# Attention and a three-way-max layer: batch 1's probabilities left unnormalised, q left unscaled, narrower last score blocks, a new order

## The chip, the cores and the metric

The kernel runs on one core of one Trainium2 chip. The metric is the device time of one execution in microseconds (us), median of three runs.

## The reference

Four batches of causal attention, 12 heads of 64 over 448 positions, feed a layer that multiplies the tokens with three 768x768 matrices, takes the maximum of the three, and multiplies with a fourth.

```python
scores = scale * np.matmul(q, k.transpose(0, 1, 3, 2))      # scale = 1/8, q and k: 4 x 12 x 448 x 64
scores = np.where(mask, -1000000000.0, scores)
scores = scores - np.max(scores, axis=-1, keepdims=True)
attn = np.exp(scores)
attn = attn / (np.sum(attn, axis=-1, keepdims=True) + 1e-09)
x = np.matmul(attn, v)                                      # rearranged to 1792 tokens x 768
h = np.maximum(np.maximum(x @ w1, x @ w2), x @ w3)
out = h @ w_out
```

All inputs and outputs are float32.

## The kernel before

Work on the attention goes by *pairs* of heads: batch b has pairs 6b to 6b + 5, and `staging` and `attend` (L680, L705) add the steps of one. `staging` loads q and k, and a second copy of parts of them with the two heads exchanged, and multiplies q by 0.125 (L699, on POOL or ACT). `attend` cuts the causal triangle into two score halves (`HALVES`), each a bank of PSUM (S, two buffers). For each half:

- PE writes the masks (bf16) and the scores (float32) with 64x64 tiles, four at a time (L724);
- DVE takes the negated maxima of two groups of blocks (L768);
- ACT takes the exp of each block with its maximum as bias, and adds up the row's sum (L780).

Then the batches part. **Batch 0** is "plain" (`PLAIN = 6` pairs): PE transposes the exps (L794), ACT copies them back, PE multiplies with v in float32 (L877), and the division comes after that. DVE takes reciprocals of the sums (L891, L892), PE copies ("spreads") them over the rows of an M bank (L898, L903), ACT evicts that (L526, hacc<-M,bsc), and DVE multiplies it with the product (`quotient`, L906). **Batches 1 to 3** divide before: the sums are scaled on ACT or DVE (`eps`, L808 or L810), DVE takes reciprocals (L814), and each of seven blocks is multiplied by its own (`sc`; L526 on ACT, L528 on DVE). Then the probabilities are split into a float16 number (`p_hi`, ACT mostly, 1024 columns) and a float16 remainder (`p_lo`, L537, POOL or DVE); SP's DMA transposes both, and PE multiplies them with v, which is split likewise (L865). In all batches the result x is split into two float16 parts (x hi, x lo).

Beside this run the layer's steps. `weight` clamps each block of the weights (ACT |w| L989, DVE L974 to L986), `split` splits it (L526 or L530, L546 or L548 and L549), `hidden` multiplies batches 0 and 1 with it (L1066, three M banks) and takes the maximum in ACT's eviction and DVE's L1081. Batches 2 and 3 go through seven products in place of eight (L1298, L1423). The projection of batches 0 and 1 is L1477.

Which step comes when, and on which engine, is set by two tables at the top of the file. `ORDER` lists the steps' numbers in the order of issue; `ENGINE` has two letters for each step. Both were found by a search with the planner in `Order.forward`, which prices each step and follows the clock of PE (`pace`, `BUSY`). Every engine runs its instructions strictly in this order. A step of POOL is made to wait for the DVE step before it if that is marked `port=True`; a DVE step is never made to wait for POOL. `RINGS` gives the number of buffers of each kind (q and k three each, hacc four, M three).

Of the kernel before, what the change touches and what calls it, by code (L numbers as in the profile page):

```python
# [7 lines left out]
F32 = mybir.dt.float32  # L8
# [7 lines left out]
P = 128  # L16
D = 64
# [9 lines left out]
PS = 2.0**14  # L27

# [6 lines left out]
ORDER = [17, 15, 0, 16, 18, 19, 47, 49, 20, 30, 21, 2, 22, 31, 23, 24, 32, 25, 50, 4, 33, 6, 34, 7, 1, 3, 26, 51, 35, 27,  # L35
# [145 lines left out]


HALVES = (
    ((4, 0, 1, 0, 384, 0), (5, 1, 1, 512, 384, 512), (0, 2, 1, 384, 128, 384), (1, 3, 1, 896, 128, 896)),
    ((2, 4, 1, 0, 256, 0), (3, 5, 1, 512, 256, 256), (6, 6, 2, 256, 256, 512)),
)

# [1422 lines left out]
```

## Time and profile before

| | before |
|---|---|
| median of 3 runs | 455.88 us (454.98 to 456.64) |
| profiled execution | 456.02 us |
| its span, first to last instruction | 454.2 us |
| busy: PE, DVE, ACT, POOL | 430.0, 415.4, 311.6, 137.1 us |
| mean granted clock | 0.989 |

The profile is of one execution; its span is the time between the first and the last instruction on the engines, and 1.8 us of the execution lie outside it. A row of the trace names the line, the engine, the operation, what it writes and reads, and its size. A line can be that of a helper: L526, L528 and L530 are the scaled copies of ACT, DVE and POOL, L537 the subtraction for a float16 remainder. "idle before" is time in which the engine did nothing just before such a row, with what ended it. The granted clock is a share of TensorE's full speed of 2.4 GHz. In time, batch 0's attention takes about the first 69 us, the first hidden matmul is at 69.63 us, batches 1 to 3 with the layer's first part follow until 312 us, then the seven products until 435 us, and the last projections.

### The profile page before, as it was taken

To read this page: it belongs to the slowest core of one execution; us is meant where nothing else is said; L and a number is where in the kernel's file an instruction comes from. 1 tells how busy PE (TensorE), PEld (TensorE's weight loads), DVE (VectorE), ACT (ScalarE), POOL (GpSimd) and SP (SyncE) were. 2 spreads that over 40 slices of the span, in tenths; PEclk is the share of its full clock that TensorE was granted. 3 is DMA by queue.
4 is the path that set the end of the run, shared out by engine and by line. 5 is a ranking of instruction groups with operands and counts; after the bars stand their busy time and mean duration, and the time that the engine had idled before them with its cause. 6 is when DMAs were issued, how large, how long until landed. Compare 5 with 4: busy or idle time off the path is not lost.

```text
span 454.2 us, 11040 instructions
## 1 busy us (share of the span) xinstructions
PE 430.0 (95%) x4277; PEld 252.6 (56%) x4277; DVE 415.4 (91%) x824; ACT 311.6 (69%) x738; POOL 137.1 (30%) x118
## 2 busy tenths in 40 slices
PE   7878878879999999999999999999999999999996
PEld 4766754435555555565666566655555555555553
DVE  2798999999999999998878999889999999999984
ACT  2899999988998989997675688883443253332510
POOL 2013433415443441722333335521123022132000
PEclk9898999989999999999999999999999999999999
DMA  7768868897889978948986687853100000000014
GB/s 216 226 206 256 261 232 217 233 224 161 207 206 176 235 249 236 202 101 173 187 166 140 137 174 143 144 114 69 42 1 0 1 1 1 1 1 20 19 43 182
DMA packets 110003, 63.62 MB, mean 140 GB/s; under 512 B 81280, under 2 KB 107392, under 8 KB 109952
## 3 DMA queue, kind: packets, MB, share of 16 engines
q1 hardware_dynamic: 101312, 50.87, 47.7%
q10 hardware_dynamic: 8640, 12.06, 8.5%
q8 instruction: 33, 0.54, 0.5%
q14 instruction: 18, 0.15, 0.1%
HBM read 38.54 MB, written 5.51 MB: 97 GB/s over the span
## 4 chain that ended last, share of the span: by engine, by line
PE 69%; ACT 12%; DVE 12%; DMA 2%; issue 2%; SPq 1%; ACTq 0%
PE M L1066 16%; PE L L1298 14%; PE M L1477 9%; PE M L1298 7%; PE S L724 6%; ACT region L526 5%; PE O L865 5%; PE L L1423 4%; ACT region L780 3%; PE O L1298 3%; PE M L1423 2%; DVE region L974 2%; DVE acc L768 2%; DVE region L982 2%; PE O L1423 2%
## 5 line engine op out<-in xcount | busy, mean ns | idle before, releaser
L1066 PE MATMUL M<-x,w 128*128 128x448 f16 x648 | 129.4, 356 | 3.9 <-DVE hacc L1081 3.2
L780 ACT ACTIVATE region<-S,acc 128x384 f32<-128x384 f32 (+3 forms) x168 | 83.1, 502 | 24.3 <-DVE acc L768 14.5
L1066 PEld LDWEIGHTS <-w 128*128 128x128 f16 x648 | 61.9, 99 | 62.7 <-issue 8.3
L537 POOL TENSOR_TENSOR region<-region 128x1024 f16<-128x1024 f32 x27 | 57.6, 2133 | 82.0 <-ACT region L526 26.4
L768 DVE TENSOR_REDUCE acc<-S 128x2 f32<-128x512 f32 (+3 forms) x96 | 63.0, 681 | 13.1 <-PE S L724 12.8
L526 ACT ACTIVATE region<-region 128x1024 f16<-128x1024 f32 (+3 forms) x59 | 45.8, 786 | 22.8 <-DVE region L1231 9.2
L526 ACT ACTIVATE region<-region,acc 128x384 f32<-128x384 f32 (+3 forms) x99 | 48.2, 525 | 6.7 <-DVE acc L814 4.4
L526 ACT ACTIVATE region<-region,cols 128x384 f16<-128x384 f32 (+1 forms) x38 | 22.8, 614 | 42.0 <-DVE region L1156 20.3
L1151 POOL TENSOR_TENSOR region<-w 128x384 f32<-128x384 f16 x21 | 19.3, 921 | 96.0 <-DVE region L546 40.7
L1298 PEld LDWEIGHTS <-region 128*128 128x128 f16 x324 | 31.7, 98 | 29.6
L724 PE MATMUL S<-region 64*64 64x256 f32 (+5 forms) x672 | 47.2, 372 | 0.7 <-DMA region<-in_k_dram 0.5
L1477 PE MATMUL M<-h,w 128*128 128x448 f16 x216 | 42.9, 353 | 0.0
L1298 PE MATMUL L<-region,region 128*128 128x448 f16 x198 | 39.4, 352 | 0.0
L1298 PEld LDWEIGHTS <-w 128*128 128x128 f16 x243 | 23.5, 98 | 21.8
L780 ACT ACTIVATION_READ_ACCUMULATOR region<-S,acc 128x1 f32 x168 | 34.4, 205 | 0.0
L1298 PE MATMUL M<-x,w 128*128 128x448 f16 x162 | 33.6, 353 | 0.0
L724 PEld LDWEIGHTS S<-region 64*64 64x64 f32 x672 | 30.4, 138 | 5.2 <-POOL region L530 0.6
L1477 PEld LDWEIGHTS <-w 128*128 128x128 f16 x216 | 20.7, 98 | 19.2 <-issue 0.3
L865 PEld LDWEIGHTS <-region 128*64 128x64 f16 x1080 | 26.4, 111 | 5.0 <-issue 4.2
L865 PE MATMUL O<-region,region 128*64 128x128 f16 (+1 forms) x1080 | 28.9, 211 | 0.0
L989 ACT ACTIVATE region<-region 128x768 f32<-128x768 f32 x24 | 22.0, 920 | 3.2 <-DMA region<-in_moe_w_out_dram 1.3
L974 DVE TENSOR_SCALAR_CACHE_REDUCE region<-region 128x768 f32<-128x768 f32 x24 | 22.5, 941 | 1.7 <-ACT region L989 1.6
(177 smaller groups left out, 779.6 us busy)
## 6 DMA issues: line engine op xcount, KB each, us to landing
region<-in_moe_w_dram SPq DMA_DIRECT2D x13, 768.0 KB, 4.7
region<-in_q_dram SPq DMA_DIRECT2D x22, 224.0 KB, 4.1
region<-in_v_dram SPq DMA_DIRECT2D x11, 384.0 KB, 5.3
region<-in_k_dram SPq DMA_DIRECT2D x18, 224.0 KB, 3.7
region<-in_moe_w_dram ACTq DMA_DIRECT2D x5, 768.0 KB, 5.1
region<-in_moe_w_out_dram ACTq DMA_DIRECT2D x3, 768.0 KB, 5.1
region<-in_moe_w_out_dram SPq DMA_DIRECT2D x3, 768.0 KB, 4.7
out_dram<-osb SPq DMA_DIRECT2D x9, 224.0 KB, 2.9
```

What stands on the lines that cost most here:

```text
L526: ACT.activation(o, i, AF.Copy, scale=f)
L537: ENG[eng].tensor_tensor(out=o, in0=i, in1=hi, op=ALU.subtract)
L724: PE.matmul(ap(o, 512 * h + dims[0], dims[1:], D * g, D), l, r, start=start, stop=True, skip_group_check=True)
L768: DVE.tensor_reduce(out=T(acc)[:, at : at + len(g)], in_=i, op=ALU.max, axis=AX.XY if parts == 2 else AX.X, negate=True)
L780: ACT.activation(o, part(T(S), parts, c, w), AF.Exp, bias=T(acc)[:, at : at + 1], accum_out=T(acc)[:, 7 + at : 8 + at])
L865: PE.matmul(T(O)[D * h : D * h + D, P * i : P * i + w], vt[j][:, vl, (2 * p + h) * D : (2 * p + h + 1) * D], queries(T(pT[u]), i, h, 8 * p ...
L974: DVE.tensor_scalar(out=T(x32), in0=T(x32), scalar1=MIN_HI, scalar2=None, op0=ALU.max, op1=ALU.max, accum_out=wmx[:, c])
L989: add([("act", c_act(DM, 0.025))], lambda e: ACT.activation(T(x32), word(1).bitcast(F32), AF.Abs), reads=[st], writes=[x32], ring=("w3", x ...
L1066: PE.matmul(T(M)[:, 0:S_LEN], w16[j][:, kk, wl, fs], xx[:, kk % 3, xl], start=(kk == 0 and wl + xl == 0), stop=(kk == 5 and wl == 1))
L1298: PE.matmul(T(M)[:, 0:S_LEN], stat(c, wl), mov(c, xl), start=first and n == 0, stop=n == 8, skip_group_check=True)
L1423: PE.matmul(T(M)[:, 0:S_LEN], stat[0](c, wl), mov[0](c, xl), start=first and c + wl + xl == 0, stop=c == 2 and wl == 1, skip_group_check=True)
L1477: PE.matmul(T(M)[:, 0:S_LEN], w16[3][:, f, wl, es], T(("h", b, f))[:, hl], start=(f == 0 and hl + wl == 0), stop=(f == 5 and wl == 1))
```

## The change

1. q is no longer scaled. The exp has `scale=0.125`, and its bias is prepared by a new small step per half (`bias`, 48 in all: 19 on ACT, 15 on POOL, 14 on DVE), between max and exp. The bias also holds ln 2^14.
2. Batch 1 leaves its exps unnormalised as batch 0 does. Its `eps`, reciprocals and seven scalings per pair are gone; reciprocals of the sums, a spread on PE, ACT's eviction and DVE's quotient per pair come in, behind the float16 product with v.
3. The last block of the second half has 224 keys for each head in place of 256 and 192. Its exp is 448 wide in place of 512, the half's p hi and p lo 960 in place of 1024; the masks follow.
4. q and k take one load each per pair; the exchanged copies come by four loads for every second pair (`kx`). The rings of q and k have two buffers; quotients have one of their own (`xr`) in place of one in the ring of hacc.
5. The planner follows the clock with a second, shifted window, and its limit is 3900 in place of 3060. `ORDER` and `ENGINE` are new throughout. Among other things 18 in place of 13 weight blocks (w hi) are scaled on ACT, and 15 in place of 9 remainders of probabilities are taken on DVE.

The core of the diff:

```diff
 RINGS = dict(
-    qr=3, kr=3, kx=1, acc=2, p32=2, ph=2, pT=3, v16=5, vr=4, w3=4, x=4, wst=2, h=6, hacc=4, osb=2, S=2, O=1, M=3,
+    qr=2, kr=2, xr=1, kx=1, acc=2, p32=2, ph=2, pT=3, v16=5, vr=4, w3=4, x=4, wst=2, h=6, hacc=4, osb=2, S=2, O=1, M=3,
...
-    BUSY = 3060
+    BUSY = 3900
...
-                rate = 2400 if cols.get(k - 1, 0.0) >= self.BUSY else 1200
+                rate = 2400 if min(cols.get(k - 1, 0.0), shifted.get(m - 1, 0.0)) >= self.BUSY else 1200
...
-        def scale(e):
-            scaled(e, T(qr), T(qr), 0.125)
...
-        add(c_scaled("q", 512), scale, writes=[qr], prio=prio, port=True)
...
                 for h, g in tiles:
-                    rows(h, g, 2 + (h != g), 0, 192 + D * (h != g))
+                    rows(h, g, 2 + g, 0, 192 + D * g)
                 for h, g in tiles:
                     hs = slice(D * h, D * h + D)
                     if h == g:
-                        m(h, g, (256, [1, 256]), qq[hs, 384:448], kk[hs, 0:256])
+                        m(h, g, (256, [1, 224]), qq[hs, 384:448], kk[hs, 224 * h : 224 * h + 224])
                     else:
-                        m(h, g, (256, [1, 192]), qq[hs, 448:512], T(kz)[hs, :])
+                        m(h, g, (256, [1, 224]), T(kz)[hs, p % 2, 0:D], T(kz)[hs, p % 2, D : D + 224])
...
+            def bias(e, z=z):
+                dims = [[4, 2], [2, 2]] if z == 0 else [[2, 3]]
+                i, o = ap(T(acc), z, dims), ap(T(acc), 16 + z, dims)
+                if e == "act":
+                    ACT.activation(o, i, AF.Identity, bias=tiny[:, 0:1], scale=0.125)
+                else:
+                    ENG[e].tensor_scalar(out=o, in0=i, scalar1=0.125, scalar2=LN_PS, op0=ALU.mult, op1=ALU.add)
+
+            add([("act", 0.19), ("dve", 0.1), ("pool", 0.2)], bias, reads=[(acc, "m", z, gi) for gi in range(2)],
+                writes=[(acc, "b", z)], prio=pr)
...
-                        o, part(T(S), parts, c, w), AF.Exp, bias=T(acc)[:, at : at + 1],
-                        accum_out=T(acc)[:, 7 + at : 8 + at])
+                        o, part(T(S), parts, c, w), AF.Exp, bias=T(acc)[:, 16 + at : 17 + at], scale=0.125,
+                        accum_out=T(acc)[:, 8 + at : 9 + at])
...
+            own = [(y, bl[0], "e") for bl in blocks]
+            if b > 1:
...
+        if b > 1:
+            f = bsc[:, b, 11:12]
...
+        f = bsc[:, b, 10:11] if plain else 1.0
+        add([("dve", 0.38)], reciprocals, reads=[(acc, "s", n) for n in range(7)], writes=[(acc, "r")], prio=prio + 0.4)
+        add([("pe", 4 * c_pe32(P) + 0.09)], spread, reads=[(acc, "r")], writes=[R], ring=("M", R), prio=prio + 0.5, mode=(2, 3))
```

The steps `eps`, its reciprocal and `sc` stand unchanged under `if b > 1`; `reciprocals`, `spread` and `quotient` are those of batch 0 and run for batches 0 and 1. Line numbers after it: max L765, bias L775 (ACT) and L777, exp L789, product with v in batch 0 L894 and later L882, reciprocals L929 and L930, spread L936 and L941, quotient L944, hidden matmul L1083, its maximum L1098, scaled copy on ACT L527, subtraction L538, clamps L991 to L1003.

PE at the end of batch 0's attention, before: the last pair's scores, its spread and its product with v, then the first hidden matmul (L1066). S and M are PSUM banks, region_61 holds probabilities, region_64 v.

```order
402 L724 MATMUL S_92<-region_65 64x64
403 L898 MATMUL M_89<-ident,acc_68 64x128 x6
404 L903 MATMUL M_89<-ident,acc_68 64x64 x2
405 L877 MATMUL O_88<-region_61,region_64 64x128 x12
406 L877 MATMUL O_88<-region_61,region_64 64x64 x8
407 L1066 LDWEIGHTS w_1_95
408 L1066 MATMUL M_90<-x_69,w_1_95 128x448
```

The same place in the change. The hidden matmuls (L1083) begin after the scores of pair 7's second half, ahead of the last product with v of batch 0:

```order
423 L1083 LDWEIGHTS w_0_93
424 L1083 MATMUL M_90<-x_68,w_0_93 128x448
425 L894 MATMUL O_87<-region_61,region_64 64x128 x12
426 L894 MATMUL O_87<-region_61,region_64 64x64 x8
427 L1083 LDWEIGHTS w_0_93
428 L1083 MATMUL M_90<-x_68,w_0_93 128x448
```

Twelve hidden matmuls now stand ahead of this product with v (L894); before, it (L877) stood ahead of all of them.

ACT in batch 1, before: scalings by a column of reciprocals (region_61<-region_61,acc_68) between evictions, and then p hi (1024 wide).

```order
170 L526 ACTIVATE region_61<-region_61,acc_68 128x128
171 L526 ACTIVATE region_61<-region_61,acc_68 128x256
172 L526 ACTIVATE h_73<-hacc_81 128x448
173 L955 DMA region_62<-in_moe_w_dram 128x6x256
174 L526 ACTIVATE region_61<-region_61,acc_68 128x512
175 L526 ACTIVATE region_61<-region_61,acc_68 128x384
176 L526 ACTIVATE region_61<-region_61 128x1024
177 L526 ACTIVATE region_61<-region_61,acc_68 128x256
```

ACT in batch 1, in the change: exps (L789), p hi straight behind them, then the copy of x (x_70<-region_65) and the eviction of spread sums (region_65<-M_89).

```order
159 L789 ACTIVATE region_61,acc_66<-S_91,acc_66 128x256 x2
160 L789 ACTIVATE region_61,acc_66<-S_91,acc_66 128x448
161 L527 ACTIVATE hacc_81<-M_90,wr 128x448
162 L789 ACTIVATE region_61,acc_66<-S_92,acc_66 128x128
163 L527 ACTIVATE region_61<-region_61 128x1024
164 L972 DMA region_62<-in_moe_w_dram 128x6x256
165 L527 ACTIVATE h_74<-hacc_80 128x448
166 L527 ACTIVATE x_70<-region_65 128x448
167 L527 ACTIVATE region_64<-region_63,bsc 128x768
168 L527 ACTIVATE region_61<-region_61 128x960
169 L527 ACTIVATE region_65<-M_89 128x448
```

The scalings have gone from between exp and p hi; the eviction of spread sums and the copy of x from region_65, before and after the quotient, are new here.

DVE around the first hidden matmuls, before: the last max of a half, `eps` of the other half (L810) and the accumulation of a hidden product (L1081).

```order
154 L986 SCALAR_TENSOR_TENSOR region_62<-region_62 128x768
155 L974 TENSOR_SCALAR region_62,wmx<-region_62 128x768
156 L768 TENSOR_REDUCE acc_67<-S_93 128x1
157 L810 TENSOR_SCALAR acc_67<-acc_67,osc 128x4
158 L1081 SCALAR_TENSOR_TENSOR hacc_82<-M_89,wr,hacc_82 128x448
159 L814 RECIPROCAL acc_67<-acc_67 128x4
160 L768 TENSOR_REDUCE acc_68<-S_92 128x2
```

DVE at about the same place in the change: a quotient (L944), a clamp step, and the addition and reciprocal of eight sums (L929, L930).

```order
150 L765 TENSOR_REDUCE acc_66<-S_92 128x1
151 L944 TENSOR_TENSOR region_65<-O_87,region_65 128x448
152 L995 TENSOR_SCALAR region_62<-region_62 128x768
153 L929 TENSOR_SCALAR acc_67<-acc_67 128x8
154 L930 RECIPROCAL acc_67<-acc_67 128x8
155 L999 SCALAR_TENSOR_TENSOR region_62<-region_62 128x768
156 L547 SCALAR_TENSOR_TENSOR w_2_95<-region_62,wf,w_2_95 128x6x128
```

`eps` is no longer ahead of L1081; a quotient and a 128x8 addition stand between the maxima and the clamps in its place.

POOL in batch 1, in the change: remainders of probabilities, now 1024 and 960 wide by turns, then the bias of a half (L777) and a remainder of x.

```order
34 L654 MEMSET region_64 64x1536
35 L538 TENSOR_TENSOR region_61<-region_61 128x1024
36 L538 TENSOR_TENSOR region_61<-region_61 128x960
37 L777 TENSOR_SCALAR acc_66<-acc_66 128x3
38 L538 TENSOR_TENSOR x_70<-region_65,x_70 128x448
```

The bias stands behind the two remainders in POOL's queue; before there was none on POOL.

## Rows read from the trace of the kernel before

**Rows 1.** The page: engines' busy time and share; granted clock in 40 slices.

```profile
PE 430.0 (95%) x4277; PEld 252.6 (56%) x4277; DVE 415.4 (91%) x824; ACT 311.6 (69%) x738; POOL 137.1 (30%) x118
...
PEclk9898999989999999999999999999999999999999
```

**Rows 2.** Windows: stretch, length, busy of PE, PEld, DVE, ACT, POOL, clock, DMA share, GB/s.

```profile
0.00:107.00 107.00, 87.09 (x1088) 59.76 (x1088) 93.17 (x193) 94.14 (x240) 33.29 (x37) 0.95 0.79 226
107.00:435.00 328.00, 327.48 (x3115) 185.05 (x3110) 309.28 (x609) 215.91 (x496) 103.81 (x82) 1.00 0.51 113
```

**Rows 3.** Windows around two falls of the granted clock.

```profile
34.00:38.00 4.00, 4.00 (x43) 2.80 (x42) 3.94 (x11) 3.36 (x11) 2.52 (x4) 0.57 0.93 335
...
99.00:103.00 4.00, 4.00 (x14) 1.72 (x13) 4.00 (x11) 4.00 (x12) 0.00 (x0) 0.57 0.69 133
```

**Rows 4.** Waits of PE up to 107 us: total, times, longest.

```profile
PE S L724 <- ACT region L780: 5.4, 5, 1.9
PE M L1066 <- DVE hacc L1081: 2.8, 1, 2.8
PE M L794 <- ACT region L780: 2.2, 3, 1.4
...
PE M L794 <- ACT region L526: 1.9, 2, 1.2
```

**Rows 5.** Timelines of POOL, DVE, PE, 96 to 104 us: start, duration, row [idle before].

```profile
96.02 2.12 POOL L537 TENSOR_TENSOR region<-region 128x1024 f16<-128x1024 f32 x1 [5.41 <-ACT region L526]
...
96.23 1.93 DVE L810 TENSOR_SCALAR acc<-acc,osc 128x4 f32<-128x4 f32 x1
...
102.58 0.22 DVE L810 TENSOR_SCALAR acc<-acc,osc 128x3 f32<-128x3 f32 x1
...
98.80 5.25 PE L1066 MATMUL M<-x,w 128*128 128x448 f16 x18 [2.80 <-DVE hacc L1081]
```

**Rows 6.** Groups on ACT: line, operation, out<-in, count | busy, mean ns | idle before.

```profile
L526 ACT ACTIVATE region<-region,acc 128x384 f32<-128x384 f32 (+3 forms) x99 | 48.2, 525 | 6.7 <-DVE acc L814 4.4
...
L526 ACT ACTIVATE w<-region,wf 128x768 f16<-128x768 f32 x13 | 11.8, 938 | 0.3 <-DVE wf L593 0.3
...
L526 ACT ACTIVATE region<-region 128x512 f32<-128x512 f32 x12 | 7.6, 633 | 0.0
...
L526 ACT ACTIVATE hacc<-M,bsc 128x448 f32<-128x448 f32 x6 | 3.9, 642 | 1.2 <-PE M L903 1.2
...
L808 ACT ACTIVATE acc<-acc,osc 128x4 f32<-128x4 f32 x9 | 2.7, 304 | 0.1
```

**Rows 7.** Timeline of PE: one pair's spread of sums in batch 0, and what follows.

```profile
44.77 0.88 PE L898 MATMUL M<-ident,acc 128*64 128x128 f32 x12 [1.44 <-DVE acc L892]
45.57 0.33 PE L903 MATMUL M<-ident,acc 64*64 64x64 f32 x4
45.83 1.09 PE L794 MATMUL M<-ident,region 128*128 128x128 f32 x8
```

**Rows 8.** Timeline of PE: a second score half in batch 0, and what follows.

```profile
49.99 0.26 PE L724 MATMUL S<-mr,ident 64*64 64x128 bf16 x4
...
50.09 0.70 PE L724 MATMUL S<-region 64*64 64x192 f32 x9
...
50.98 1.09 PE L794 MATMUL M<-ident,region 128*128 128x128 f32 x8
```

**Rows 9.** Groups on DVE and POOL.

```profile
L906 DVE TENSOR_TENSOR hacc<-O,hacc 128x448 f32<-128x448 f32 x6 | 3.7, 610 | 0.0
...
L891 DVE TENSOR_SCALAR acc<-acc 128x7 f32<-128x7 f32 x6 | 1.5, 258 | 0.0
...
L537 POOL TENSOR_TENSOR region<-region 128x1024 f16<-128x1024 f32 x27 | 57.6, 2133 | 82.0 <-ACT region L526 26.4 <-DVE region L528 21.3 <-issue 8.6
...
L530 POOL TENSOR_SCALAR region<-region 128x512 f32<-128x512 f32 x12 | 7.4, 617 | 33.4 <-DMA region<-in_q_dram 14.2 <-DVE region L986 5.7 <-DVE region L528 5.6
```

**Rows 10.** The page's DMA issues: KB each, median us from issue to landing.

```profile
region<-in_k_dram SPq DMA_DIRECT2D x18, 224.0 KB, 3.7
```

More of the change, by code (lines that the diff above doesn't have):

```diff
@@ L804, in attend @@
                 continue
-            def eps(e, cols=cols):
-                if e == "act":
-                    ACT.activation(cols(14), cols(7), AF.Identity, bias=tiny[:, 0:1], scale=1.0 / PS)
-                else:
-                    DVE.tensor_scalar(
-                        out=cols(14), in0=cols(7), scalar1=1.0 / PS, scalar2=tiny[:, 0:1], op0=ALU.mult, op1=ALU.add)
-            add([("act", 0.19), ("dve", 0.1)], eps, reads=[(acc, "s", bl[0]) for bl in blocks], writes=[(acc, "t", z)], prio=pr)
@@ L814, in attend, with flat @@
[L814 to L823 removed]
+            def flat(t, n, z):
+                return t.rearrange("p a b -> p (a b)")[:, 1024 * n : 1024 * n + 1024 - D * z]
@@ L825, in p_hi @@
             def p_hi(e, z=z, y=y):
[L826 removed]
+                scaled(e, flat(T(ph[z]), 0, z), T(y)[:, 0 : 1024 - D * z], 1.0)
             def p_lo(e, z=z, y=y):
[L829 to L833 removed]
@@ L834, in attend, with cols, eps, sc @@
-            add(c_rest("p lo", 1024), p_lo, reads=[(ph[z], 0)] + [(y, bl[0]) for bl in blocks], writes=[(ph[z], 1)], prio=pr,
-                port=True)
+                rest(e, flat(T(ph[z]), 1, z), T(y)[:, 0 : 1024 - D * z], flat(T(ph[z]), 0, z))
+            own = [(y, bl[0], "e") for bl in blocks]
+            if b > 1:
+                def cols(c, z=z):
+                    return ap(T(acc), c + z, [[4, 2], [2, 2]] if z == 0 else [[2, 3]])
+                def eps(e, cols=cols):
+                    if e == "act":
+                        ACT.activation(cols(16), cols(8), AF.Identity, bias=tiny[:, 1:2], scale=1.0 / PS)
+                    else:
+                        DVE.tensor_scalar(
+                            out=cols(16), in0=cols(8), scalar1=1.0 / PS, scalar2=1e-9, op0=ALU.mult, op1=ALU.add)
+                add([("act", 0.19), ("dve", 0.1)], eps, reads=[(acc, "s", bl[0]) for bl in blocks], writes=[(acc, "t", z)], prio=pr)
+                add([("dve", 0.09)], lambda e, cols=cols: DVE.reciprocal(cols(24), cols(16)), reads=[(acc, "t", z)],
+                    writes=[(acc, "r", z)], prio=pr)
+                for n, at, parts, c, w, d in blocks:
+                    def sc(e, at=at, d=d, n=parts * w, y=y):
+                        t = T(y)[:, d : d + n]
+                        scaled(e, t, t, T(acc)[:, 24 + at : 25 + at])
+                    add(c_scaled("p late" if b >= LATE else "p", parts * w, False), sc, reads=[(y, n, "e"), (acc, "r", z)],
+                        writes=[(y, n)], prio=pr, port=True)
+                own = [(y, bl[0]) for bl in blocks]
@@ L837, in attend @@
+            add(c_scaled("p hi late" if b >= LATE else "p hi", 1024 - D * z), p_hi, reads=own, writes=[(ph[z], 0)],
+                ring=("ph", ph[z]), prio=pr, port=True)
+            add(c_rest("p lo", 1024 - D * z), p_lo, reads=[(ph[z], 0)] + own, writes=[(ph[z], 1)], prio=pr, port=True)
             od.group = f"t{6 * b + p}"
@@ new lines, in reciprocals, with spread @@
+        def reciprocals(e):
+            a = T(acc)
+            DVE.tensor_scalar(out=a[:, 16:24], in0=a[:, 8:16], scalar1=1e-9 * PS, scalar2=None, op0=ALU.add)
+            DVE.reciprocal(a[:, 24:32], a[:, 16:24])
+        def spread(e):
+            a = T(acc)
+            for i in range(3):
+                for h in range(2):
+                    PE.matmul(
+                        T(R)[D * h : D * h + D, P * i : P * i + P], ap(a, 24 + i + 4 * h, [[0, D]]), queries(ident, i, h, 0),
+                        start=True, stop=True)
+            for h in range(2):
+                hs = slice(D * h, D * h + D)
+                PE.matmul(T(R)[hs, 384:448], ap(a, 27, [[0, D]], D * h, D), ident[hs, hs], start=True, stop=True)
```

232 lines of the change are left out of this document (106 added, 126 removed), and 184 rows, old and new, of the table ORDER.

## The prediction

> **What bounds the kernel now.** I read the page's shares first, then the windows, then PE's waits and a timeline. PE is busy 430.0 us of a span of 454.2 [rows 1], so 24.2 us are idle. The windows show where. Up to 107 us PE is busy 87.09 us, which leaves 19.9 idle; from 107 to 435 us it is busy 327.48 of 328, which leaves 0.5 [rows 2]. The rest, 3.8 us, is at the end, mostly the output's eviction and store, which the change does not touch. So two things set the time: the sum of PE's own work, and what PE loses before 107 us. To those 19.9 idle us belongs a second loss. The granted clock falls to its lower level, 1.2 GHz, in three slices of the page's clock line [rows 1]; in two of the windows of 4 us around them the mean is 0.57 [rows 3], which is some 3.4 us at half speed in 4, or 1.7 us lost each time, 5.1 in all. In the third case PE had stood still for 2.80 us just before [rows 5]. PE's loss up to 107 us is thus 19.9 + 5.1 = 25.0 us.
>
> Who keeps PE waiting there? Mostly ACT: 5.4 + 2.2 + 1.9 = 9.5 us of waits end with an exp or an eviction [rows 4]. The largest single wait ends with DVE's accumulation of the hidden layer, 2.8 us [rows 4], and its cause is one instruction. DVE's L810, a scaling of 128x4 numbers, starts at 96.23 us while POOL is in a 1024-wide subtraction from 96.02 to 98.14, and ends only with it: 1.93 us, where the same kind of instruction at 102.58 us takes 0.22 [rows 5]. Everything behind it on DVE is 1.7 us late, PE stands still, and the clock then falls: 2.8 + 1.7 = 4.5 us for one small instruction.
> The Trainium skill, SBUF — State Buffer, section Who interferes with whom, has a rule for this: DVE and GpSimd share a port pair, the first to issue holds it for its whole instruction, and the other blocks completely; tensor_scalar in a two-port mode is named among what takes it. The trace agrees with it, 1.93 against 0.22 us.
>
> **The change, part by part.**
> *Spread on PE, added.* Six pairs of batch 1 now divide by the sums after the product with v, so PE must copy each pair's reciprocals over the rows, as it already does in batch 0. There it takes from 44.77 to 45.83 us until the next matmul, 1.06 us, and at least the 0.88 us of its main part [rows 7]. Batch 1 lies mainly where PE has no idle time (second row of [rows 2]), so nothing hides it: 6 x 1.06 = **+6.4 us**, bounds 5.3 and 6.4.
> *Last block 224 wide.* Per pair the score columns stay at 1792, and 24 mask matmuls go (336 to 312). Four masks stand in the 0.1 us between 49.99 and 50.09 us [rows 8], with two narrow ones beside them, so one costs about 17 ns: **-0.4 us**. The four tiles had 448 columns each; now two have 416 and two 480. If the longest sets the end, 32 of 448 columns of the 0.9 us from 50.09 to 50.98 [rows 8] are 0.06 us, over 24 pairs +1.4; if the lower tile's extra mask columns had been the longest, up to -1.4. I take 0, between the two, and keep both ends. The exp and p rows it shortens lie on ACT and POOL and are counted below.
> *ACT.* Its scalings of probabilities fall from 99 to 57, and one takes 525 ns on average [rows 6]: 22 us less. It loses 12 scalings of q on either engine, of which its own are 633 ns [rows 6]. It gains six evictions of the spread sums (642 ns [rows 6]), 19 of the 48 new bias instructions (nearest row: the 128x4 eps, 304 ns [rows 6]) and five weight scalings that the order moves to it from POOL (938 ns [rows 6]). What matters is what stands ahead of PE in the early part. I took the second score half of pair 9, at 106.11 us in the trace, and counted in the two orders which rows each engine must have finished before it. PE's own work ahead of it is the same within 0.5 us. ACT has 18 scalings less (-9.5), four q scalings less (-2.5), two weight scalings more (+1.9), two passes over weights or v fewer (each near the weight scaling's 938 ns, -1.8), and -0.3 of small items: 12 us by durations, 9 if each row is taken to overlap the next by the 0.1 us that DVE's rows show (the one at 96.23 ends 0.08 us after the next begins [rows 5]).
> *DVE.* Over the whole of batch 1 it is even: six quotients more (610 ns [rows 9]) against six subtractions for x, of nearly that length, that go mostly to POOL; 6 pairs of a 128x8 addition and reciprocal (258 ns for the nearest addition [rows 9]) and 14 bias instructions (0.22 us) against twelve small reciprocals and thirteen eps. Ahead of pair 9's second half, though, it has three weight remainders and four clamp steps less, since the order puts them later: 6 us less.
> *Bias, added to the chain.* Each half now waits between max and exp for a small instruction: on DVE 0.22 to 1.93 us by L810 [rows 5], on ACT 304 ns [rows 6], on POOL at most the 617 ns of the q scaling [rows 9], and there it can queue behind a 2133-ns subtraction [rows 9]. Behind a waiting exp stand the next evictions on ACT, and PE waits for those. I take 0.2 us, by the undisturbed L810, since the order puts most beside the max on the same or an idle engine; at the ten waits of the first 107 us that end with an exp or eviction [rows 4] it is +2.0.
> *Loads.* Six transfers per pair become two and, every second pair, four; SP issues 118 instead of 164, ACT about six more. The rings of q and k go from three to two, so a load waits until the scores of the pair before last are done; it then lands in 3.7 us [rows 10], and pairs follow one another about every 10 us in batch 0. Cost 0 under that cover. If transfers slipped by a pair, every score half would wait for some of these 3.7 us. The single buffer for quotients makes the next pair's sums wait for the last x remainder on POOL; pairs are far enough apart, and if not, one of PE's three M banks is held and the next hidden matmul waits.
>
> **Sum.** PE's loss before 107 us is 25.0. The L810 collision goes, since eps is no longer in batch 1: -4.5 (the DVE excerpt has no such row there; new small rows may collide, see below). Of ACT's 9.5 us of waits at most 6 can go, because then DVE, only 6 us earlier itself, is the later of the two; less 2.0 for the bias, -4.0. Together -8.5, bounds 0 (all of it is given back) and -10.5 (bias hidden). The profiled execution took 456.02 (span 454.2 and 1.8 around it). 456.02 + 6.4 - 0.4 - 8.5 = 453.5; the median of the runs is 0.14 lower than this execution, and I leave the forecast at **453.5 us**. A measurement of this kernel tells about 0.3% from no change, that is 1.4 us, so "same" is 454.5 to 457.2.
>
> **Rivals.**
> 1. *More is gained early.* The bias is hidden beside other work, the clock does not fall a third time and tile lengths cost nothing: -10.5 and a spread of 0.88: 456.0 + 5.3 - 0.4 - 10.5 = 450.4. For it: PE in the new order has hidden matmuls to do from pair 7 on, where it now waits for scores. Against it: DVE had only 14 us idle in 107. Chance 0.12; my own forecast 0.42.
> 2. *The bias is on the path in all twenty halves before 107 us*, not in ten: +4.4 instead of +2.0, so the loss falls by 6.1: 456.0 + 6.0 - 6.1 = 455.9, no change. For it: the waits for exp are the largest group [rows 4]. Against: only ten waits stand in twenty halves. Also here: DVE becomes the late engine and gives only half of its 6 us. Chance 0.24.
> 3. *Slower: a new collision with POOL.* Batch 0 and 1 now have 21 short additions or scalings on DVE (bias and sums) ahead of the place where PE is ahead for good, against 9 before, and none is kept apart from POOL by the planner. POOL now does mainly 2-us subtractions [rows 9] in that stretch. The point from which it decides: one starts over a microsecond before POOL's instruction ends, and PE has no matmuls queued. Then the 4.5 us are not gained, 0.4 us of chain is lost besides: 456.0 + 6.0 - 4.0 + 0.4 = 458.4. Two such cost another 4.5. For it: the row at 96.23 us [rows 5]. Against it: most of the 9 rows before were hit for 0.2 us or not at all, and PE's new order keeps matmuls at hand from pair 7 on. Chance 0.22.
> The rule of the Trainium skill, SBUF — State Buffer, Who interferes with whom, would let each of the 21 block; how often they meet a POOL row no run here shows yet.
>
> That the change does not do what it says is part of rival 2: fewer ACT passes help only while ACT is the late engine, and after 107 us it is not.
>
> **How the numbers follow.** Faster: forecast and rival 1, 0.54. Same: 0.24. Slower: 0.22. The likeliest case alone spans 451.5 to 455.5. The range reaches from rival 1, less a part of the 1.4 us of tile lengths (449.5), to rival 3 with 1 us on top (459.5); it leaves out a second collision and a gain beyond DVE's 6 us.
>
> **What would show it.** PE busy rises by 5 to 6 us with 72 more spread matmuls; the time PE loses up to the last wait falls from 25 to about 16 or 17; the waits for exp fall to half; no half-clock stretch near 100 us; ACT's busy time falls by about 20 us and DVE's stays. It is wrong if PE still waits 20 us or more before its last wait, if a DVE row of 128x8 or 128x4 lasts over 1 us there, if PE waits after 120 us, for an x or a DMA, or if one score half takes longer than 1.05 us.

## The result and the profile after

The change takes 461.17 us in the median (456.74 to 465.49) against 455.88: ratio 1.0113, 95% interval 1.009 to 1.0136. It is slower by 5 us; forecast were 453.5 in a range up to 459.5. Medians here are of all runs, while ratios and their intervals leave out executions more than 1.5% above a kernel's fastest, so the two can differ a little.

The profiled execution of the change took 460.37 us, its span is 458.6. Its page, the engines' busy time and the granted clock:

```profile
PE 435.6 (95%) x4349; PEld 254.5 (55%) x4349; DVE 414.8 (90%) x825; ACT 303.1 (66%) x723; POOL 133.6 (29%) x125
...
PEclk9799999999999999999999999899999999999999
```

PE has 5.6 us more than in [rows 1] and 72 rows more: 96 for the 48 spread matmuls, each of which is two rows of the trace, less 24 masks. ACT has 8.5 us less, not about 20. The clock line now has a dip late, in the 26th slice. The windows of the change, the first two as in [rows 2] (the stretch, its length, busy time of PE, PEld, DVE, ACT and POOL, granted clock, DMA):

```profile
0.00:107.00 107.00, 93.70 (x1212) 64.09 (x1213) 95.41 (x206) 91.38 (x240) 37.62 (x41) 0.97 0.83 225
107.00:435.00 328.00, 322.04 (x3034) 180.29 (x3033) 303.37 (x592) 207.04 (x475) 94.95 (x83) 0.99 0.52 114
280.00:312.00 32.00, 29.63 (x354) 17.40 (x353) 27.07 (x53) 22.01 (x57) 9.87 (x7) 0.95 0.81 143
```

The account goes as in the prediction. Up to 107 us PE is idle for 13.3 us, and a mean clock of 0.97 is some 3.2 us lost at half speed: 16.5, where the kernel before lost 25.0. After 107 us it is idle for 6.0 us, and in the third window a clock of 0.95 over 32 us is another 1.6: 7.6, where the kernel before lost 0.5.

| us | before | change | difference |
|---|---|---|---|
| PE's work at full clock (busy less half-speed loss) | 424.9 | 430.8 | +5.9 |
| lost up to 107 us (idle and half clock) | 25.0 | 16.5 | -8.5 |
| lost from 107 to 435 us | 0.5 | 7.6 | +7.1 |
| idle at the end | 3.8 | 3.7 | -0.1 |
| span | 454.2 | 458.6 | +4.4 |

In this account of one execution each, PE's added work and the loss up to 107 us came as the prediction said, and the error is the third line. PE's waits from 107 to 435 us in the change (in total, times, longest):

```profile
PE O L882 <- DMA region<-region: 4.0, 3, 2.4
PE M L936 <- DVE acc L930: 1.5, 1, 1.5
PE M L1083 <- DVE hacc L1098: 0.4, 1, 0.4
```

The first is the product with v, which waits for transposed probabilities. Where it is longest, the timeline of PE:

```profile
287.72 1.08 PE L882 MATMUL O<-region,region 128*64 128x128 f16 x36 [2.37 <-DMA region<-region]
```

and of SP's queue and of POOL just before (start, duration, row):

```profile
270.69 1.84 SPq L857 DMA_TRANSPOSE region<-region  x1
275.45 1.34 SPq L692 DMA_DIRECT2D region<-in_q_dram  x2
276.83 2.14 SPq L692 DMA_DIRECT2D region<-in_k_dram  x2
279.07 0.54 SPq L698 DMA_DIRECT2D region<-in_q_dram  x1
279.78 7.64 SPq L857 DMA_TRANSPOSE region<-region  x2
...
273.67 2.02 POOL L538 TENSOR_TENSOR region<-region 128x960 f16<-128x960 f32 x1
```

POOL has the remainder of probabilities ready at 275.69. Its transposes are issued only from 279.78 on, since five loads of the next pairs stand ahead of them on SP; the four of L692 had themselves waited for a buffer of exchanged copies until 275.45. The first of these transposes then takes 7.9 us from issue to landing, where the median of the 36 is 5.3, and PE starts as it lands: the wait has two parts, a late issue and a slow landing. Near 97 us the same two kinds of row are late again, with a wait of POOL ahead of them:

```profile
97.08 1.04 POOL L538 TENSOR_TENSOR x<-region,x 128x448 f16<-128x448 f32 x1 [5.98 <-DVE acc L929]
98.07 4.11 POOL L538 TENSOR_TENSOR region<-region 128x1024 f16<-128x1024 f32 x2
...
97.93 1.35 SPq L692 DMA_DIRECT2D region<-in_q_dram  x2
99.33 1.72 SPq L692 DMA_DIRECT2D region<-in_k_dram  x2
101.16 0.53 SPq L694 DMA_DIRECT2D region<-in_k_dram  x1
101.79 6.85 SPq L857 DMA_TRANSPOSE region<-region  x2
```

POOL stood for 5.98 us before a remainder of x, with the remainder of pair 8's probabilities behind it (what that order costs, experiment 7 shows). PE waits for these transposes for 1.43 us at 109.17. The second wait of the list is a collision of DVE with POOL:

```profile
137.44 1.87 DVE L929 TENSOR_SCALAR acc<-acc 128x8 f32<-128x8 f32 x1
139.35 0.20 DVE L930 RECIPROCAL acc<-acc 128x8 f32<-128x8 f32 x1
...
137.16 2.13 POOL L538 TENSOR_TENSOR region<-region 128x1024 f16<-128x1024 f32 x1 [4.48 <-ACT region L1006]
...
139.60 0.88 PE L936 MATMUL M<-ident,acc 128*64 128x128 f32 x12 [1.48 <-DVE acc L930]
...
18.20 0.15 DVE L929 TENSOR_SCALAR acc<-acc 128x8 f32<-128x8 f32 x1
```

The same addition takes 0.15 us at 18.20, with POOL idle beside it, and 1.87 where it starts 0.28 us into POOL's subtraction and ends with it. The rule in the Trainium skill, SBUF — State Buffer, Who interferes with whom (the first of DVE and GpSimd to take their shared port pair blocks the other), agrees with both rows.

### The profile page after: what moved, and what is told of

Same layout as the page of the kernel before. It is cut to its first block, busy times and chain, and to the rows that moved or that the text cites. A ratio compares the mean times of both kernels' runs of the same rounds, so it can differ in the third digit from the quotient of the medians.

```text
span 458.6 us, 11085 instructions
## 1 busy us (share of the span) xinstructions
PE 435.6 (95%) x4349; PEld 254.5 (55%) x4349; DVE 414.8 (90%) x825; ACT 303.1 (66%) x723; POOL 133.6 (29%) x125
## 2 busy tenths in 40 slices
DMA packets 109236, 64.03 MB, mean 140 GB/s; under 512 B 80512, under 2 KB 106624, under 8 KB 109184
## 5 line engine op out<-in xcount | busy, mean ns | idle before, releaser
L1083 PE MATMUL M<-x,w 128*128 128x448 f16 x648 | 127.9, 353 | 1.6 <-ACT region L527 1.1
L789 ACT ACTIVATE region<-S,acc 128x384 f32<-128x384 f32 (+3 forms) x168 | 81.6, 496 | 28.9 <-DVE acc L777 7.5
L1083 PEld LDWEIGHTS <-w 128*128 128x128 f16 x648 | 61.2, 98 | 59.1 <-issue 4.3
L765 DVE TENSOR_REDUCE acc<-S 128x2 f32<-128x768 f32 (+1 forms) x96 | 60.8, 663 | 8.9 <-PE S L719 8.5
L538 POOL TENSOR_TENSOR region<-region 128x960 f16<-128x960 f32 (+1 forms) x21 | 43.3, 2064 | 67.7 <-ACT region L527 28.3
L527 ACT ACTIVATE region<-region 128x1024 f16<-128x1024 f32 (+3 forms) x51 | 40.2, 800 | 29.2 <-DVE region L1248 7.9
L719 PE MATMUL S<-region 64*64 64x224 f32 (+6 forms) x768 | 49.5, 363 | 2.7 <-DMA region<-in_k_dram 2.7
L527 ACT ACTIVATE region<-region,cols 128x384 f16<-128x384 f32 (+1 forms) x38 | 22.6, 611 | 35.0 <-DVE region L1173 24.4
L719 PEld LDWEIGHTS S<-region 64*64 64x64 f32 x768 | 32.8, 137 | 8.9 <-issue 4.6
L1315 PE MATMUL L<-region,region 128*128 128x448 f16 x180 | 36.5, 352 | 0.0
L789 ACT ACTIVATION_READ_ACCUMULATOR region<-S,acc 128x1 f32 x168 | 34.7, 206 | 0.0
L882 PE MATMUL O<-region,region 128*64 128x128 f16 (+1 forms) x1080 | 29.5, 211 | 4.0 <-DMA region<-region 4.0
L882 PEld LDWEIGHTS <-region 128*64 128x64 f16 x1080 | 26.9, 111 | 11.0 <-issue 10.8
L1315 PE MATMUL M<-x,w 128*128 128x448 f16 x162 | 32.9, 353 | 0.0
L527 ACT ACTIVATE region<-region,acc 128x384 f32<-128x384 f32 (+3 forms) x57 | 28.4, 528 | 1.5 <-DVE acc L838 1.4
L991 DVE TENSOR_SCALAR_CACHE_REDUCE region<-region 128x768 f32<-128x768 f32 x24 | 22.6, 941 | 2.3 <-ACT region L1006 2.2
```

Source lines behind the costliest of these rows:

```text
L527: ACT.activation(o, i, AF.Copy, scale=f)
L538: ENG[eng].tensor_tensor(out=o, in0=i, in1=hi, op=ALU.subtract)
L719: PE.matmul(ap(o, 512 * h + dims[0], dims[1:], D * g, D), l, r, start=start, stop=True, skip_group_check=True)
L765: DVE.tensor_reduce(out=ap(T(acc), at, [[4, len(g)]]), in_=i, op=ALU.max, axis=AX.XY if parts == 2 else AX.X, negate=True)
L789: ACT.activation(o, part(T(S), parts, c, w), AF.Exp, bias=T(acc)[:, 16 + at : 17 + at], scale=0.125, accum_out=T(acc)[:, 8 + at : 9 + at])
L882: PE.matmul(T(O)[D * h : D * h + D, P * i : P * i + w], vt[j][:, vl, (2 * p + h) * D : (2 * p + h + 1) * D], queries(T(pT[u]), i, h, 8 * p ...
```

## The experiments

Every ratio is to the kernel before on the same chip; 1% is 4.55 us. "Below the change" or "below the ninth" is the difference of two ratios; with both intervals it is good to some 1.6 to 2.5 us.

**1. Copies behind the transposes.** The order of SP, as ahead of the wait at 288 us; the same was done with five such groups in all.

```diff
-L692 DMA region_65<-in_q_dram 64x2x64 x2
-L692 DMA region_65<-in_k_dram 64x2x224 x2
-L698 DMA region_65<-in_q_dram 128x448
 L857 DMA_TRANSPOSE region_61<-region_61 128x16x128
+L692 DMA region_65<-in_q_dram 64x2x64 x2
+L692 DMA region_65<-in_k_dram 64x2x224 x2
+L698 DMA region_65<-in_q_dram 128x448
 L857 DMA_TRANSPOSE region_61<-region_61 128x16x128
```

> The change, with five loads of exchanged copies (from batch 1 on) put behind the next transpose in SP's queue; every other engine's order is the same. Theory A (late transposes: from 107 us on PE is early, the transposes of the probabilities stand in SP's queue behind these loads, which wait for PE's scores, and PE waits for them): PE's waits for DMA region fall from 4.0 us to 1.5 or less, and the time falls by 1.5 to 4 us against the change, to 457 to 459.5. Theory B (short DVE instructions blocked by POOL) and theory C (only the added work on PE counts): 461, within 0.7.

Measured: 459.97 us, 1.0100 (1.0062 to 1.0137), 0.6 us below the change and so not told from it. The wait at 288 us is gone, but the one near 113 has grown:

```profile
101.87 1.95 SPq L857 DMA_TRANSPOSE region<-region  x1
103.92 1.64 SPq L692 DMA_DIRECT2D region<-in_q_dram  x2
...
116.08 1.49 PE L882 MATMUL O<-region,region 128*64 128x128 f16 x36 [2.73 <-DMA region<-region]
```

Now SP stands before a transpose that waits for POOL, and the loads behind it, and the next transpose behind them, are late.

**2. No addition.** The addition of 1e-9 to the sums (L929) is left out.

```diff
-            DVE.tensor_scalar(out=a[:, 16:24], in0=a[:, 8:16], scalar1=1e-9 * PS, scalar2=None, op0=ALU.add)
-            DVE.reciprocal(a[:, 24:32], a[:, 16:24])
+            DVE.reciprocal(a[:, 24:32], a[:, 8:16])
```

> The change without the addition of 1e-9 to the sums (the 12 L929 instructions); DVE takes the reciprocals of the sums straight, which the collision of L929 with POOL at 137.44 us (1.87 us) cannot hold. Theory B: PE's wait for L930 at 139.6 us (1.48) goes, and the 12 instructions with it: 1.5 to 2.5 us less, 458.7 to 459.7. Theory A and C: at most 0.5 us less, since the later waits for transposes take back what is gained.

Measured: 459.25 us, 1.0063 (1.0028 to 1.0098), 2.3 us below the change. The wait for L930 after 107 us is gone. So, in this execution, is the wait at 288 us, although SP's order is that of the change (SP's timeline, then PE's waits after 107 us):

```profile
277.48 6.32 SPq L857 DMA_TRANSPOSE region<-region  x2
...
PE O L882 <- DMA region<-region: 0.8, 1, 0.8
```

The transposes stand behind the same five loads, but the first of them lands in 5.8 us in place of 7.9, and PE does not wait. The loads ahead take away the margin; whether PE then stands depends on the landing too. In runs 3, 5 and 6, with SP's order of the change, PE stood there for 2.0 to 3.1 us; in the profiled runs with the order of experiment 1 (1, 7 to 11, 15) it did not.

**3. Most of batch 1's spread left out.** Six of the eight matmuls of each pair, 36 of 48, are left out (the two of L941 stay), and the eviction scales by 2^-40.

```diff
-            for i in range(3):
+            for i in range(3 if plain else 0):
```

> The change without batch 1's 48 spread matmuls; ACT evicts a bank with old content, scaled to nothing, so batch 1's result has no meaning; all else runs as in the change. Theory C (the loss is the added PE work): 6.4 us less, 454.8, and PE's waits as before. Theory A: PE reaches the transposes earlier and waits for part of it: 3 to 5 us less, 456 to 458, and the waits for DMA region grow above 4.0 us.

Measured: 458.17 us, 1.0072 (1.0045 to 1.0099), only 1.9 us below the change. By the rows of the spread some 4.8 us of PE's work are gone (0.8 us a pair). PE's idle time after 107 us is 8.0 us in place of 6.0, but its waits for transposes did not grow as theory A had it: 3.3 us, 4.0 in the change.

**4. Kernel before without scalings.** The seven multiplications of batch 1's probabilities are left out.

```diff
                 def sc(e, at=at, d=d, n=parts * w, y=y):
+                    if b == 1:
+                        return
```

> The kernel before, with its own order, without the seven scalings per pair of batch 1's probabilities (its result is then not normalised). If ACT is the late engine before 107 us, as the prediction has it, its relief alone lets PE's waits for exps and evictions fall by 4 to 6 us: 450 to 452. If DVE and its collision with POOL decide, less than 1.5 us: 454.5 to 456.

Measured: 455.01 us, 1.0005 (0.9979 to 1.0032): nothing. The window up to 107 us:

```profile
0.00:107.00 107.00, 86.14 (x1094) 59.21 (x1095) 94.34 (x194) 87.38 (x224) 33.64 (x37) 0.95 0.80 227
```

PE's waits in it:

```profile
PE S L724 <- ACT region L780: 6.6, 6, 1.9
PE M L1068 <- DVE hacc L1083: 2.8, 1, 2.8
```

ACT is 6.8 us less busy than in [rows 2], but DVE's wait of 2.8 us stands as in [rows 4], and the waits for exp do not shrink. In the order of before, a lighter ACT is worth nothing that the runs can tell while that collision stands.

**5. First copies on SP.** One step's engine, in `ENGINE`.

```diff
-"spacspacspacpospdvdvpedvdvdvdvspspacpedv
+"spacspacspacpospdvdvpedvdvdvdvspspsppedv
```

> Edit: the exchanged copies of the first pair of heads are loaded by SP's queue in place of ACT's; nothing else moves. In the change's trace PE waits 0.88 us at 7.9 us and 1.80 us at 10.3 us for these copies, and the clock is at its lower level afterwards. Theory (part of the loss is the way the loads are issued at the start): both waits shrink to 0.5 us or less in sum, and the time falls by 1.5 to 2.5 us against the change. Rival (the start is hidden, since batch 0 is limited by DVE anyway): the same PE waits come back at the next max or exp, and the time falls by under 0.5 us.

Measured: 462.64 us, 1.0177 (1.0127 to 1.0227). It is 2.9 us above the change, over four runs. The waits for copies are gone; PE then stands 2.7 us for DVE's L641 (2.0 in the change) and 3.0 for exps ahead of scores (1.6). The theory fell: other waits, for DVE and ACT, took the place of the one removed. What made it slower, no run shows.

**6. Bias on ACT.** 29 steps' letters in `ENGINE` become `ac`.

> Edit: all 48 bias steps run on ACT, where the exp that needs them runs; 14 leave DVE and 15 leave POOL. Theory A (short DVE rows held up by POOL and steps queued behind POOL's subtractions are what is lost): DVE's L777 rows, with 5.6 us of excess over 0.25 us in the change, are gone, POOL's queue is freer, and the time falls by 1 to 3 us. Theory B (the loss after 107 us is SP's queue and POOL's remainders of probabilities): the transposes stay late, PE's waits on DMA stay at 3 to 4 us, and the time moves by under 1 us. Rival (ACT is the late engine): 29 more rows of 0.3 us on ACT, 9 us, make it slower by 2 us or more.

Measured: 465.06 us, 1.0216 (1.0167 to 1.0265), 4.7 us above the change. The rival was right in sign: the spread of batch 0's last pair starts at 66.48 us, in the change at 64.02, so 2.46 us later. PE's waits from 107 to 150 us grew on top:

```profile
PE O L882 <- DMA region<-region: 3.5, 1, 3.5
PE M L936 <- DVE acc L930: 2.1, 1, 2.1
```

**7. Remainder first.** The first experiment, and in POOL's order:

```diff
-L538 TENSOR_TENSOR x_70<-region_65,x_70 128x448
 L538 TENSOR_TENSOR region_61<-region_61 128x1024
+L538 TENSOR_TENSOR x_70<-region_65,x_70 128x448
```

> Edit: as in the run with the copies behind the transposes (the first experiment), and POOL takes the remainder of pair 8's probabilities ahead of the remainder of pair 6's x, for which it waited 6 us in the change. Theory (two heads of queues, SP's and POOL's, together make the transposes late): the wait of L882 near 110 to 116 us goes (2.7 us in the first experiment, 1.4 in the change) as does that at 288 us; DMA waits of PE fall to 1.5 us or less, and the time to 1.5 to 3 us below the change's. Rival (the remainder of x is late next, or DVE is): the wait moves to a row of the maxima or a product with x, and the time is within 0.7 us of the first experiment's.

Measured: 457.29 us, 1.0057 (1.0019 to 1.0095), 2.5 us below the change. Its window from 107 us:

```profile
107.00:435.00 328.00, 325.02 (x3058) 181.95 (x3057) 307.45 (x600) 210.73 (x483) 95.08 (x83) 1.00 0.52 113
```

What is left of the wait for transposes in it:

```profile
PE O L882 <- DMA region<-region: 1.0, 1, 1.0
```

SP's timeline near 275 us, where the transposes now stand ahead of the loads:

```profile
271.27 8.30 SPq L857 DMA_TRANSPOSE region<-region  x2
279.62 1.70 SPq L692 DMA_DIRECT2D region<-in_q_dram  x2
```

PE's idle time after 107 us falls from 6.0 to 3.0 us, and the late half clock is gone.

What POOL's new order adds to the first experiment isn't shown. The remainder of probabilities, now first, still stands:

```profile
97.46 2.14 POOL L538 TENSOR_TENSOR region<-region 128x1024 f16<-128x1024 f32 x1 [6.22 <-DVE acc L929]
```

Its p hi was ready at 94.69. The wait ends with DVE's L929 (97.31), right behind DVE's copy of x (97.23); most likely it is the planner's rule that a step of POOL waits for the DVE step before it. So the remainder starts 0.6 us earlier than in the change, not 6. And the profiled execution of experiment 1 was 1.65 us behind this one already at batch 0's last spread (65.68 and 64.03 us), ahead of any row that either edit moves; the ratios of 1 and 7 differ by 2.0 us, with 2.4 of uncertainty.

**8. All together.** Experiments 2 and 5 to 7 in one.

> Edit: all of them: copies of the first pair on SP, later copies behind the transposes, pair 8's remainder of probabilities ahead of pair 6's x, bias on ACT alone, and no separate addition to the sums (its 1e-9 is left out). Theory (the change's losses are separate and add up): -2 start, -2 addition, -2 to -3 queues, -1 bias: 453 to 455 us, at or below the kernel before. Rival (DVE and the order of steps limit the first 107 us, so that a wait taken away is replaced by the next): 457 to 459.

Measured: 462.31 us, 1.0152 (1.0124 to 1.018). It is slower still than the rival's 457 to 459: two of the four parts (5 and 6) cost time by themselves.

**9. Remainder first, no addition.** Experiments 7 and 2.

> Edit: the run with pair 8's remainder first (seventh experiment), and the sums' separate addition of 1e-9 left out (second experiment; beside sums of at least 2^14 it is below half a unit of the last place of a float32). Theory (the two losses are separate: the late transposes cost 2.5 us and the DVE addition that POOL held up 2.0 us): 454.5 to 456 us, ratio 0.998 to 1.002, PE's waits after 107 us 1.5 us or less. Rival (as with all edits together, they don't add up, since the order shifts): 457 to 459 us, PE waiting 3 us or more after 107 us.

Measured: 453.95 us, 0.9975 (0.9947 to 1.0004), 6.3 us below the change. Most of the late losses are gone:

```profile
0.00:107.00 107.00, 93.93 (x1243) 63.91 (x1244) 94.84 (x200) 93.09 (x243) 37.72 (x41) 1.00 0.85 232
107.00:435.00 328.00, 326.16 (x3042) 182.27 (x3041) 306.85 (x601) 209.85 (x480) 94.86 (x83) 1.00 0.50 112
```

Idle are 13.1 and 1.8 us, both at full clock. The time is that of the forecast, 453.5, but not by its sum: the additions that are left out were part of the change, and this execution lost nothing to the lower clock early (13.1 up to 107 us, where the forecast had 16.5).

**10. The ninth without the spread** (edit of the third).

> Edit: as the run beside it (remainder first, no addition), and the spread matmuls of batch 1 are left out (its outputs are then scaled by 2^-40 instead of divided). Theory (the spread is on the path for its full length once nothing else is late, my term of 6.4 us): 5 to 6.4 us below the run beside it, 449 to 450.5. Rival (what stands behind a removed spread is late anyway, as in the third experiment, where only 1.9 of 4.4 us came): 2 us or less below it.

Measured: 453.51 us, 0.9968 (0.9943 to 0.9992): 0.3 us. Again 36 of the 48 matmuls are gone. The windows from 70 to 145 us of the ninth, then of this run:

```profile
70.00:145.00 75.00, 72.58 (x893) 43.08 (x892) 71.20 (x143) 60.41 (x139) 33.00 (x24) 1.00 1.00 226
```

```profile
70.00:145.00 75.00, 69.97 (x841) 40.40 (x835) 72.41 (x141) 61.31 (x139) 32.82 (x24) 1.00 1.02 228
```

PE's largest waits in this run's window:

```profile
PE M L1082 <- DVE hacc L1097: 1.7, 2, 1.3
PE M L1082 <- ACT region L527: 1.1, 2, 0.7
```

PE and DVE are both nearly full there, 72.6 and 71.2 of 75 us. Without these matmuls PE idles 5.0 us in place of 2.4, mostly in waits for DVE and ACT. The two executions can't be compared further: at batch 0's last spread, which no edit touches, this one is already 2.2 us late (63.46 and 61.24 us), having lost some 5 us to the lower clock in its first 36 us, where the ninth lost none. The 0.3 us stand on twelve runs each, and are good to 1.7.

**11. Scalings back on ACT.** On the ninth:

```diff
-            def p_hi(e, z=z, y=y):
+            def p_hi(e, z=z, y=y, blocks=blocks):
+                for n, at, parts, c, w, d in blocks if b == 1 and e == "act" else ():
+                    scaled("act", T(y)[:, d : d + parts * w], T(y)[:, d : d + parts * w], 1.0)
```

> Edit: as the run with the remainder first and no addition, but ACT multiplies each of batch 1's 42 blocks of exps by 1.0 in place ahead of p hi, as many passes of some 0.5 us as the change took away (about 21 us on ACT, 9 to 10 of them ahead of the second half of pair 9). Theory of the prediction (ACT relief ahead of pair 9's second half is worth 4 us on the path): slower by 3 to 5 us, with PE's waits that end with an exp or eviction up by as much before 110 us. Rival (as the fourth experiment says of the kernel before: ACT was not the late engine): within 1 us.

Measured: 458.80 us, 1.0072 (1.005 to 1.0095), 4.4 us above the ninth by the ratios. PE's largest wait up to 107 us, an ACT row ahead of a hidden matmul:

```profile
PE M L1084 <- ACT region L527: 3.4, 2, 2.5
```

So in the ninth's order, which is nearly the change's, ACT's relief is worth 4.4 us; the prediction had at most 6, before it took 2.0 off for the bias.

**12. Kernel before without DVE's scalings of sums** in batch 1.

```diff
-            def eps(e, cols=cols):
+            def eps(e, cols=cols, z=z):
+                if b == 1 and e == "dve":
+                    gone.add((p, z))
+                    return
```

> Edit: the kernel before, without the scalings of the sums on DVE in batch 1 (L810; the reciprocals then take the raw sums, so batch 1's probabilities are too small by 2^14). Theory of the prediction (the L810 row at 96 us, held up by POOL, costs 2.8 us of waiting and 1.7 us of half clock): 4 to 4.5 us below the kernel before, no PE wait of 2.8 us at 98.8 us. Rival (the engines behind are late anyway, so that another wait takes its place): within 1.5 us of the kernel before.

Measured: 451.76 us, 0.9922 (0.9891 to 0.9952): 3.5 us.

**13. One of them moved to ACT.** The kernel before, one step's letters in `ENGINE` (`dv` to `ac`).

> Edit: the kernel before with one step moved: the scaling of four sums that DVE held from 96.23 to 98.16 us (L810) runs on ACT, 304 ns by the row of L808. All other steps stay; the result is that of the reference. Theory (that one row's collision with POOL is what the twelfth experiment took away, 3.4 us): 3 to 4 us below the kernel before, about 452, PE's wait of 2.8 us at 98.8 us gone. Rival (the twelfth experiment gained by the other DVE scalings that it left out too, or ACT is late there): less than 1.5 us.

Measured: 452.09 us, 0.9947 (0.9923 to 0.997), 2.4 us faster than the kernel before. It is faster than the change too. Its timelines of DVE, POOL and ACT at the place of [rows 5]:

```profile
94.86 0.67 DVE L1081 SCALAR_TENSOR_TENSOR hacc<-M,wr,hacc 128x448 f32<-128x448 f32 x1
...
94.64 2.13 POOL L537 TENSOR_TENSOR region<-region 128x1024 f16<-128x1024 f32 x1 [5.39 <-ACT region L526]
...
94.41 0.29 ACT L808 ACTIVATE acc<-acc,osc 128x4 f32<-128x4 f32 x1
```

Its window around 99 us:

```profile
95.00:103.00 8.00, 7.41 (x88) 4.17 (x88) 7.73 (x19) 7.97 (x20) 3.36 (x2) 1.00 0.78 191
```

The accumulation runs beside POOL's subtraction at its usual length, and the half-clock stretch of [rows 3] near 99 us is gone.

**14. Spread in the kernel before.** Eight matmuls ahead of the second part of each product with v of batch 1.

```diff
+            if b == 1 and z == 1:
+                r = T(acc)
+                for i in range(3):
...
+                            T(O)[D * h : D * h + D, P : 2 * P], ap(r, 21 + (2, 4, 0)[i] + h, [[0, D]]),
```

> Edit: the kernel before, with the spread matmuls of six pairs put into batch 1 ahead of the second part of each product with v, into a stretch of O that the product then overwrites: 48 matmuls of the spread's shapes and nothing that waits for them. Theory A (my term: PE's order is full there, so each spread costs 0.88 to 1.06 us): 5 to 6.4 us slower. Theory B (as the tenth experiment, in which leaving them out gave 0.4: up to some 145 us DVE and ACT set the pace and PE's added work lies in its waits): 2 us slower or less, since only the last two pairs come where PE has no waits.

Measured: 461.49 us, 1.0122 (1.0086 to 1.0158): 5.5 us slower. Five of the six pairs' matmuls run after 107 us (112.50 to 168 us), the first at 104.10. The window from 107 us stays full, so these lie on the path:

```profile
107.00:435.00 328.00, 327.41 (x3180) 186.42 (x3179) 307.43 (x603) 215.65 (x496) 102.78 (x80) 1.00 0.51 112
```

**15. The ninth with most of the spread twice.**

```diff
-            for i in range(3):
+            for i in (0, 1, 2) if plain else (0, 1, 2, 0, 1, 2):
```

> Edit: the run with the remainder first and no addition (ninth experiment), with six of the eight spread matmuls of each pair of batch 1 issued twice: 36 more, 0.8 us a pair, 4.8 us in all. Theory A (PE sets the pace in batch 1): 4 to 5 us slower than the ninth, 458 to 459. Theory B (DVE and ACT set it up to some 145 us): 2 us slower or less, 456 or below.

Measured: 456.33 us, 1.0036 (1.0016 to 1.0056): 2.8 us above the ninth by the ratios, between the theories. Of 4.8 us added, three fifths show.

## Why the prediction was wrong

- **The loss after 107 us, and *Loads*, "Cost 0 under that cover"**: this step failed. The sum has no term for PE's loss from 107 to 435 us; it took over the 0.5 us of the kernel before without a reason, although the order is new throughout. In the change that stretch lost 7.6 us. It held 4.0 us of waits for transposes, 1.5 for the sums' addition, 0.4 for a hidden product and 1.6 of lower clock. The loads of a pair did land in time, and apart from the start no score half waited long for them. But the step on loads asked only who waits for a load, and not what is queued behind it. Ahead of 288 us five loads, four of them held by the single buffer of exchanged copies, kept the transposes from SP for 4 us, and a landing of 7.9 us did the rest. Reordering SP and POOL together returned 2.5 us (7), with the additions left out 6.3 (9), and no row of PE's own work had to change. SP's order alone gave 0.6, which is not clear of noise (1), and the share of each of the two queues stays open.
- **Spread, +6.4.** About right for a PE that has no idle time: 5.5 in the order of before (14), and PE's work rose by 5.9 with the masks. In the change's order its marginal price is less: in the ninth, 0.3 for some 4.8 us taken away and 2.8 for 4.8 added, each good to 1.7. The premise "Batch 1 lies mainly where PE has no idle time" holds for half of it: three of the six spreads start before 107 us (77.46, 95.96 and 104.22), where PE idles, while experiment 14 put five of its six behind. DVE is besides nearly as full as PE up to 145 us. Which of the two counts for more, no run shows.
- **The collision, -4.5.** The mechanism was right, the size too big: 2.4 (1.4 to 3.5) with that row alone moved (13), 3.5 (2.2 to 5.0) with all of its kind in batch 1 left out (12).
- **ACT, -4.0 net of the bias.** 4.4 without the bias in the ninth's order (11), against 0 in that of before (4). What makes the difference, the collision's end or the new order, was not tried apart. The bias has no price of its own here: moving it all to ACT (6) changed ACT's load and the waits behind it at once. ACT's busy time fell by 8.5 us, not by the 20 of the signs: the prediction's own terms add up to some 15, and the new order moves further passes (over v and the outputs) to ACT.
- **Tile lengths, 0**: borne out. A second score half takes 1.00 us from its first mask to the next product (57.72 to 58.72 us), before 0.99 [rows 8].
- **The early loss, 25.0 to 16.5**: measured 16.5. That it agrees so closely is luck. In runs 1, 2, 3, 7, 9 and 10, which have nearly the same order up to 107 us, the same sum gives 13.1 to 19.2, since stretches at the lower clock in the first 36 us came from no time to three times.
- **Rival 3** named a new collision with POOL. It came, at 137.44 us, with 1.48 us of waiting, and was one fifth of the late loss. Two more came early, L929 for 1.29 us at 35.67 and 1.17 at 45.84, each ending with a row of POOL (L550); PE stood no more than 0.9 us behind either, and the early loss fell as forecast. The rival's counter-argument, that PE's new order keeps matmuls at hand, did not hold at 137.44. Both signs of failure came: these rows of over 1 us, and a wait for a DMA after 120 us, the row at 287.72.

Not tried: POOL's new order alone, the queues' order with the loads kept as before, the 224-wide blocks alone, the bias alone, and a second buffer for the exchanged copies.

## What to carry to other kernels

When a change merges loads or cuts a ring of buffers, list for every in-order queue (SP and POOL too) what stands behind the instruction that may now wait, and follow that to the engine that sets the end. A stretch without idle time keeps that property only as long as its order and queues do, so a new order needs its own account there. Work added to an engine costs its full length only where the engine has no idle time and no second engine is as full: look up where each of the new rows will run, and read both from the windows before any run. And before a profile is compared with another, look at a row that no edit touches: if it is already late there, the two executions differ by chance.

## What the runs showed of the hardware that was not expected

- After a stop of PE of 2.37 us at 287.72 us the granted clock fell: its mean from 280 to 312 us is 0.95, a mix of the two levels, 1.2 and 2.4 GHz, or some 1.6 us lost on top. Without a stop there (7, 9) the clock after 107 us is 1.00. But a stop need not bring a fall: in experiment 3 PE stood 2.83 us at the same place, and the clock from 280 to 312 us is 1.00.
- One DVE row of 128 x 4 numbers moved to ACT, 0.29 us of work, made a kernel of 455 us faster by 2.4 us.
- A transpose takes longer in the change, 5.3 us from issue to landing in the median of 36, against 4.5 before, with DMA 99% busy from 70 to 145 us against 91%. One and the same transpose, behind the same five loads near 280 us, landed in 5.8 us (2), 7.9 (the change) and 9.2 (3).
